# A loop over expert jobs: half of the next expert's first matrix is split a job ahead, its squares two jobs ahead, and its weights are asked for in two jobs

## The chip, the cores and the metric

The kernel runs on one core of one Trainium2 chip. The metric is the device time of one execution in microseconds (us), the median of several runs. The profile is one execution taken by the hardware profiler on that core. PE is TensorE (PEld its weight loads), DVE is VectorE, ACT is ScalarE, POOL is GpSimd, and SP is SyncE, which here only issues DMAs and reads registers.

## The reference, cut to what matters

```python
# attention: 4 x 8 heads, 768 tokens, head size 48
for t in range(S):
    cur = einsum('bhd,bhe->bhde', u * k_t, v_t)
    y_t = einsum('bhd,bhde->bhe', r_t, state + cur)
    state = w * state + einsum('bhd,bhe->bhde', k_t, v_t)
# mixture of experts on x = y as 3072 rows of 384; 8 experts, hidden size 1024
logits = x @ w_gate + modality_bias[modality_id]
e_idx = argmax(logits); gate_w = softmax(logits)[e_idx]
for e in range(E):
    h = maximum(x[mask] @ w1[e], 0.0)
    out[mask] = gate_w * (h @ w2[e])
```

The bias decides nearly all of the choices. With these inputs three experts have tokens: 1569, 1354 and 149.

## The kernel before, in words

**Attention and the first expert.** For about 200 us the attention runs in 24 units, and between them the kernel sends each token's row to a table in DRAM by expert and works off tiles of 128 rows of the first expert (`s_up`, `s_high`, `s_low`, `s_down`). What is left over is put into a table of jobs by `jobs()` (lines 837 to 947): a chain of small DVE instructions, drawn on piece by piece between other work, which ends in a product `jd`, a PE matmul `ptab` (line 939) and the copy to `tab`. A job is 128 rows of one expert. For each job the table holds the first row of its tokens (ROW), which expert to load (MORE) and a code: 4 says that the expert changes at this job, 8 that it changes at the next one, and 1 that the job is the one ahead of a change to the third or a later expert.

**The numbers.** Matrices are float32 in DRAM and are used as a pair of float16: `whi` (ACT, `broad`, line 1019) and the remainder `wlo` (DVE, `rest`, line 1023), both scaled by a power of two that comes from the sum of squares of the weights (`ws` for the first matrix, `wsb` for the second). `raw` holds the float32 weights of the next expert: columns 0 to 3071 are the first matrix, the rest the second. Activations are pairs too: `hh` (ACT, `relu_high`, line 1084) and `hl` (DVE, `relu_low`, line 1088). `F0 // 3` is 512 columns, `F0` 1536, `F2` 1920, `WC` 3072.

**The loop** (line 1660) goes over jobs 1 to 13 here, job 0 stands ahead of it (lines 1605 to 1622). Every engine runs its own program through the loop, in the written order; only SP, ACT and DVE take the branches. A job on PE is three groups of the first product (`raise_`, line 1074: features 0 to 3, 4 and 5, 6 and 7; for each, the `whi` terms come first and the `wlo` terms after them; 72 matmuls of 128 columns) with the small matmul `pw` (line 982, it sums the squares) behind the second group, then 16 matmuls of 384 columns of the second product (`high_terms`, line 1150; `wlo` of features 5 to 7 come last), and, at the top of the next round, 8 more with `hl` (`low_terms`, line 1158). In this order a round does:

- `finish_up()`: `relu_low` of features 4 to 7 of the job before (DVE).
- `take_in`: POOL copies the activations `xn` that a DMA has brought to `mxT` and the row numbers `mn` to `mt`. `turn` (line 1064): SP asks for `xn` of the job after this one.
- At a change, `go_on()`: the rest of the first matrix is split. In the job ahead of a change to the third expert, `by_both`: three of six squares on ACT, three on DVE.
- `low_terms` and `put` of the job before (ACT scales the result to `otb`, POOL scatters it to `out`).
- At a change, the first 1920 columns of the second matrix (`undo` writes `wf`, then blocks of 960). Then `due` (lines 1216 and 1217: `fac`, `ids`), `raise_` and `relu_high` of the first group, `raise_` of the second, `pw`.
- At a change, the last 1152 columns of the second matrix, and `relu_low` of features 0 to 3 behind them; in every other job `relu_low` and the five small instructions from the sums to `ws` and `wsb`.
- `next_load`: SP asks for both halves of the expert after this one, once the splits have read `raw`.
- `relu_high` of the second group, `raise_` and `relu_high` of the third, `begin()` if the next job is a change (the first 512 columns of `whi`), and `high_terms`.

```python
for g, span in enumerate(spans): ...         # job 0
with tc.For_i(1, nj, 1, ...) as i, ...:
    finish_up()
    take_in(nc.gpsimd)
    self.turn(0, self.at(ROW, i, E * CAP, SP, 1), mn, xn)
    with tc.If(code % 8 > 3) as begun:
        go_on()
    with begun.Else():
        with tc.If(code % 2 > 0):
            by_both(squares)
    self.low_terms(po)
```

Here job 0 and job 1 belong to the first expert, job 2 is the change to the second (11 jobs, 2 to 12), job 13 the change to the third, whose last 64 or fewer rows follow behind the loop as a half job (`h_up("z", ...)` and what follows, lines 1696 to 1712).

Of the kernel before, what the change touches and what calls it, by code (L numbers as in the profile page):

```python
# [18 lines left out]
P = 128  # L19
# [6 lines left out]
E = 8  # L26
# [43 lines left out]
class _Kernel:  # L70
# [766 lines left out]
    def jobs(self):  # L837
# [77 lines left out]
        v.reduce_sum(f, eq[:, :, 1:], axis=AX.X)  # L915
        v.reduce_sum(g, eq[:, :, 2:], axis=AX.X)
        yield
        v.scalar_tensor_tensor(field[:, SEEN : SEEN + 1], jr[:, 0:1], self.linep, field[:, ROW : ROW + 1], ALU.add, ALU.subtract)

# [4 lines left out]
        b = new("jbit", [P, 1])  # L924
        v.scalar_tensor_tensor(b, f[:, now], 4.0, g[:, soon], ALU.mult, ALU.add)
        mr = new("mr", [P, E - 1])
        v.tensor_mul(mr, eq[:, 1, 1:], nx[:, 1:])
# [291 lines left out]
    def run(self):  # L1219
# [386 lines left out]
        for g, span in enumerate(spans):  # L1606
            self.raise_(ph[g], *span)
            self.relu_high(ph[g], *span)
            if g == 0:
                self.relu_low(ph[g], *span)  # L1610
                self.scales("1")

        def finish_up():
            for g in (1, 2):
                self.relu_low(ph[g], *spans[g])

# [12 lines left out]
        def blocks(m, *at):  # L1629
            for lo, hi in zip(at, at[1:]):  # L1630
                self.broad(m, lo, hi)
                self.rest(m, lo, hi)

        def begin():
            self.broad(0, 0, F0 // 3)

        def go_on():
            self.rest(0, 0, F0 // 3)
            blocks(0, F0 // 3, F0, F0 + F0 // 2, WC)

# [7 lines left out]

        def next_load():
            more = self.at(MORE, i, 2 * E - 1, SP)  # L1650
            with tc.If(more > 0):
                self.load(more % E, 2, 0, 1)

# [6 lines left out]
        with tc.For_i(1, nj, 1, iteration_sync="reg_based") as i, tc.manual_schedule(engines={getattr(mybir.EngineType, e) for e in MS[:4]}):  # L1660
            finish_up()
            take_in(nc.gpsimd)
            self.turn(0, self.at(ROW, i, E * CAP, SP, 1), mn, xn)
            code = self.at(CODE, i, 15, AD)
            with tc.If(code % 8 > 3) as begun:
                go_on()
# [4 lines that stand above are left out]
            self.put(po, 0, "b")  # L1671
            with tc.If(code % 8 > 3):  # L1672
                self.undo()
                blocks(1, 0, F2 // 2, F2)
            self.due(m2, i)
            self.raise_(ph[0], *spans[0])
            self.relu_high(ph[0], *spans[0])
            self.raise_(ph[1], *spans[1])
            scaled = self.scales_("2")
            next(scaled)  # L1680
            with tc.If(code % 8 > 3) as first:
                blocks(1, F2, WC)
                self.relu_low(ph[0], *spans[0])
            with first.Else():
                self.relu_low(ph[0], *spans[0])
                for _ in scaled:
                    pass
                nc.vector.tensor_copy(self.wsb, self.ws[:, 1:])
            next_load()
            self.relu_high(ph[1], *spans[1])  # L1690
            self.raise_(ph[2], *spans[2])
            self.relu_high(ph[2], *spans[2])
            with tc.If(code > 7):
                begin()
            self.high_terms(po)
        take_in(nc.vector)
        finish_up()
        xhalf = self.xT[:, :, HP:P]
# [57 lines left out]
```

## Time and profile before

| | us |
|---|---|
| median of 3 runs | 330.07 (329.5, 331.53, 330.07) |
| the profiled execution: its own time | 330.74 |
| its span, first to last instruction | 329.0 |
| PE busy | 316.3 (96%) |
| DVE, POOL, ACT busy | 216.5, 186.8, 159.4 |
| the loop, from the first matmul of job 1 to the first behind the loop | 210.29 to 318.13 |

The granted TensorE clock was 0.99 on average and 1.00 in all of the loop. The span is what the rows below add up to; 1.74 us of the execution's own time lie outside it. Times within a row are from the start of the span.

### The profile page before, as it was taken

Reading aid. Unit: us, or ns where it says so; the run is one execution under the profiler, and the core shown is the slowest. Engines: PE = TensorE matmul, PEld = TensorE weight load, DVE = VectorE, ACT = ScalarE, POOL = GpSimd, SP = SyncE. Lnnn points to the kernel's source line nnn. Section 1 sums busy time; section 2 is a strip of 40 time slices with the busy share of each in tenths; the row PEclk is TensorE's granted clock in tenths of the full one; section 3 lists DMA queues with packets and bytes.
Section 4 is the critical chain, followed back from the end, with each engine's and each line's share of the span. In section 5 each row is a group of like instructions: output and inputs, shape, how many; then the busy total and the mean of one; then the engine's idle time right before and its main releaser. Section 6 shows DMA issues by size and latency. Waiting matters only on the chain. (4 is left out here: it accounts for less than half of the span.)

```text
span 329.0 us, 13842 instructions
## 1 busy us (share of the span) xinstructions
PE 316.3 (96%) x5056; PEld 259.2 (79%) x5056; DVE 216.5 (66%) x705; ACT 159.4 (48%) x380; POOL 186.8 (57%) x298
## 2 busy tenths in 40 slices
PE   7999999989999999999999999999999999999983
PEld 3888888889797988879789688876688888887652
DVE  6987789795999899978768841276222223336780
ACT  4667677662367546657834341283222222226731
POOL 8997698954999897656377723234323322222212
PEclk9999999998999999999999999999999999999998
DMA  7869688959949954899978332119822212221100
GB/s 214 251 174 303 188 248 269 185 109 243 339 121 221 283 178 90 180 272 258 202 155 260 114 87 57 35 44 339 122 60 48 48 48 48 60 57 26 48 16 28
DMA packets 50748, 49.59 MB, mean 151 GB/s; under 512 B 35573, under 2 KB 44315, under 8 KB 50448
## 3 DMA queue, kind: packets, MB, share of 16 engines
q1 hardware_dynamic: 46480, 37.93, 48.5%
q0 software_dynamic: 3168, 9.47, 8.3%
q10 hardware_dynamic: 1056, 1.58, 1.4%
q8 instruction: 30, 0.49, 0.7%
q14 instruction: 14, 0.11, 0.1%
HBM read 30.55 MB, written 11.44 MB: 128 GB/s over the span
## 5 line engine op out<-in xcount | busy, mean ns | idle before, releaser
L1082 PEld LDWEIGHTS <-whi 128*128 128x128 f16 x1248 | 71.0, 99 | 4.8 <-issue 2.0
L1156 PEld LDWEIGHTS <-hh 128*128 128x128 f16 x384 | 36.1, 98 | 24.1 <-issue 1.8
L1082 PE MATMUL phb<-mxT,whi 128*128 128x128 f16 x672 | 44.5, 219 | 1.0 <-POOL mxT L1620 0.8
L1091 DVE SCALAR_TENSOR_TENSOR hl<-phb,hh 128x256 f16<-128x256 f32 (+1 forms) x42 | 20.1, 509 | 34.7 <-PE pw L982 17.9
L1082 PEld LDWEIGHTS <-wlo 128*128 128x128 f16 x624 | 37.0, 99 | 0.3 <-DVE wlo L1025 0.3
L380 POOL TENSOR_TENSOR rc<-ud,powr 112x512 f32<-112x512 f32 x23 | 30.4, 1323 | 9.3 <-DMA ud<-in_pd 9.2
L1086 ACT ACTIVATE hh<-phb 128x256 f16<-128x256 f32 (+1 forms) x42 | 18.8, 453 | 30.8 <-PE L1082 12.5
L682 POOL DMA_INDIRECT rows<-row,posi x24 | 26.1, 1089 | 10.7 <-issue 9.1
L1082 PE MATMUL phs<-mxT,whi 128*128 128x128 f16 x480 | 31.1, 223 | 0.9 <-DMA mxT<-rows 0.9
L458 DVE TENSOR_TENSOR at<-psc,mask 128x512 f32<-128x512 f32 x48 | 31.6, 680 | 0.1
L452 PE MATMUL psc<-rc,kc 64*128 64x128 f32 (+1 forms) x384 | 28.6, 285 | 0.8 <-DVE rc L380 0.4
L1161 PEld LDWEIGHTS <-hl 128*128 128x128 f16 x192 | 18.4, 98 | 13.6 <-issue 1.7
L564 ACT ACTIVATE row<-py,sx 128x384 f16<-128x384 f32 x24 | 13.9, 581 | 30.4 <-DVE sx L338 22.5
L452 PEld LDWEIGHTS psc<-rc,kc 64*128 64x128 f32 (+1 forms) x384 | 23.7, 187 | 3.8 <-issue 1.7
L1050 POOL TENSOR_TENSOR seenb<-otb,putb 128x1 int32<-128x1 int32 x13 | 3.8, 295 | 39.7 <-ACTq L1672 31.0
L487 PE MATMUL py<-kv,at 128*64 128x48 f32 x768 | 26.4, 222 | 0.0
L1156 PE MATMUL po<-wlo,hh 128*128 128x384 f16 x112 | 25.2, 326 | 1.1 <-DVE wlo L1025 1.1
L1082 PE MATMUL phb<-mxT,wlo 128*128 128x128 f16 x336 | 25.8, 219 | 0.2 <-DVE wlo L1025 0.2
L487 PEld LDWEIGHTS py<-kv,at 128*64 128x64 f32 x768 | 25.0, 138 | 0.5
L1620 POOL COPY mxT<-xn 128x768 f16<-128x768 f16 x13 | 10.8, 828 | 25.5 <-PE L1156 17.9
L1156 PE MATMUL po<-whi,hh 128*128 128x384 f16 x112 | 25.1, 326 | 0.0
L1039 ACT ACTIVATE otb<-po,fac 128x384 f32<-128x384 f32 x13 | 7.5, 577 | 34.8 <-PE phb L1082 31.6
(317 smaller groups left out, 690.5 us busy)
## 6 DMA issues: line engine op xcount, KB each, us to landing
ud<-in_pd SPq DMA_DIRECT2D x24, 384.0 KB, 4.9
kv<-in_pt SPq DMA_DIRECT2D x24, 384.0 KB, 4.6
raw<-in_w SPq DMA_DIRECT2D x12, 512.0 KB, 4.9
raw<-in_w SPq DMA_DIRECT2D x2, 1536.0 KB, 7.6
r<-in_pt SPq DMA_DIRECT2D x10, 192.0 KB, 6.2
rows<-pad ACTq DMA_DIRECT2D x1, 1544.0 KB, 6.8
rows<-row,posi POOLq DMA_INDIRECT x24, 5.0
xn<-rows SPq DMA_TRANSPOSE x14, 3.0
```

The costliest lines, as they stand in the source:

```text
L380: return (engine or nc.gpsimd).tensor_mul(u["rc"][:R, s], u["rT"][:, s], self.powr[:R, s])
L452: nc.tensor.matmul(u["ps"][j][:, pr * P : (pr + 1) * P], u["kc"][r, pr, :], u["rc"][r, pr, :], start=True, stop=True)
L458: return nc.vector.tensor_mul(u["at"][:, j * NPR : (j + 1) * NPR, :], u["ps"][j].rearrange("p (q t) -> p q t", q=NPR), self.mask.unsqueeze ...
L487: nc.tensor.matmul(py[t, sl], u["at"][:, j * NPR + pr, t], u["v"][:, sl], start=c == h == 0, stop=h == H - 1 and i >= BARE, skip_group_che ...
L564: self.nc.scalar.activation(u["x16"][:, :DM], u["x"], AF.Copy, scale=u["g"]["sx"][:, b : b + 1])
L682: i = nc.gpsimd.indirect_dma_start(out=self.rows, out_offset=bass.IndirectOffsetOnAxis(ap=u["posi"][:, b : b + 1], axis=0), in_=u["row"][: ...
L1082: self.nc.tensor.matmul(ph[:, q * n : (q + 1) * n], w[:, c0 : c0 + P], x[:, xq, :], start=i == q == 0, stop=i == len(terms) - 1, skip_grou ...
L1086: self.nc.scalar.activation(self.hh[:, f0 : f0 + fb, t * P : (t + 1) * P], p3, AF.Relu)
L1091: self.nc.vector.scalar_tensor_tensor(self.hl[:, f0 : f0 + fb, r], p3, 0.0, self.hh[:, f0 : f0 + fb, r], ALU.max, ALU.subtract)
L1156: self.nc.tensor.matmul(po[:, :DM], self.hh[:, f, t * P : (t + 1) * P], w[:, c0 : c0 + DM], start=n == 0, stop=False)
L1161: self.nc.tensor.matmul(po[:, :DM], self.hl[:, f, t * P : (t + 1) * P], self.whi[:, c0 : c0 + DM], start=False, stop=f == FB - 1)
L1620: take_in = lambda e: (e.tensor_copy(self.xT[:, :, :P], xn), e.tensor_copy(m2[:, 0, :], mn[:, 0, :]))
```

## The change

The table's code says 1 two jobs ahead of a change if the expert in between has more than three jobs (`far`), else one job ahead as before. `relu_low` of features 4 to 7 stands in its own round. `begin()` splits 1536 columns, `whi` and `wlo`, in the job ahead of a change, and `go_on()` only the other 1536. `pw` stands behind the third group, and the scales are worked out only in the job with the squares. The first half of an expert's weights is asked for in the job of the change, the second half in the job after it, behind that job's `turn`.

```diff
         v.reduce_sum(g, eq[:, :, 2:], axis=AX.X)
-        yield
+        dq, far = new("dq", [P, E - 2]), new("far", [P, 1])
+        v.tensor_sub(dq, eq[:, 3, 2:], eq[:, 2, 2:])
+        yield
+        v.scalar_tensor_tensor(dq, jc[:, 1 : E - 1], 3.5, dq, ALU.is_gt, ALU.mult)
+        yield
+        v.reduce_sum(far, dq, axis=AX.X)
...
         v.scalar_tensor_tensor(b, f[:, now], 4.0, g[:, soon], ALU.mult, ALU.add)
+        yield
+        v.tensor_add(b, b, far)
...
             self.relu_high(ph[g], *span)
+            self.relu_low(ph[g], *span)
             if g == 0:
-                self.relu_low(ph[g], *span)
                 self.scales("1")
...
         def begin():
-            self.broad(0, 0, F0 // 3)
+            blocks(0, 0, F0 // 3, F0)
         def go_on():
-            self.rest(0, 0, F0 // 3)
-            blocks(0, F0 // 3, F0, F0 + F0 // 2, WC)
+            blocks(0, F0, F0 + F0 // 2, WC)
...
-        def next_load():
-            more = self.at(MORE, i, 2 * E - 1, SP)
+        def next_load(job, half):
+            more = self.at(MORE, job, 2 * E - 1, SP)
             with tc.If(more > 0):
-                self.load(more % E, 2, 0, 1)
+                self.load(more % E, 2, half)
...
-            finish_up()
             take_in(nc.gpsimd)
             self.turn(0, self.at(ROW, i, E * CAP, SP, 1), mn, xn)
+            next_load(i - 1, 1)
             code = self.at(CODE, i, 15, AD)
...
             self.raise_(ph[1], *spans[1])
+            with tc.If(code % 8 > 3):
+                blocks(1, F2, WC)
+            self.relu_low(ph[0], *spans[0])
+            next_load(i, 0)
+            self.relu_high(ph[1], *spans[1])
+            self.raise_(ph[2], *spans[2])
             scaled = self.scales_("2")
             next(scaled)
-            with tc.If(code % 8 > 3) as first:
-                blocks(1, F2, WC)
-                self.relu_low(ph[0], *spans[0])
-            with first.Else():
-                self.relu_low(ph[0], *spans[0])
+            self.relu_high(ph[2], *spans[2])
+            self.relu_low(ph[1], *spans[1])
+            self.relu_low(ph[2], *spans[2])
+            with tc.If(code % 2 > 0):
                 for _ in scaled:
                     pass
                 nc.vector.tensor_copy(self.wsb, self.ws[:, 1:])
-            next_load()
-            self.relu_high(ph[1], *spans[1])
-            self.raise_(ph[2], *spans[2])
-            self.relu_high(ph[2], *spans[2])
             with tc.If(code > 7):
                 begin()
             self.high_terms(po)
         take_in(nc.vector)
-        finish_up()
```

## Rows read from the trace of the kernel before

**Rows 1.** Busy time by stretch; one stretch per job, columns headed in the first line.

```profile
core 0: us, PE busy (x) PEld busy (x) DVE busy (x) ACT busy (x) POOL busy (x), PEclk, DMA share, GB/s
...
218.24:227.62 9.38, 8.66 (x99) 6.25 (x98) 8.60 (x12) 5.98 (x9) 4.98 (x4) 1.00 0.57 195
227.62:236.51 8.89, 8.11 (x98) 6.40 (x97) 2.33 (x10) 2.46 (x5) 2.24 (x5) 1.00 0.96 212
...
244.46:252.40 7.94, 7.94 (x98) 6.39 (x97) 2.33 (x10) 1.95 (x4) 2.28 (x5) 1.00 0.20 47
...
300.07:308.60 8.53, 8.16 (x99) 6.31 (x97) 5.98 (x16) 5.54 (x10) 2.61 (x5) 1.00 0.20 48
308.60:318.13 9.53, 7.65 (x92) 5.56 (x90) 8.35 (x11) 6.73 (x10) 1.83 (x2) 1.00 0.04 12
```

**Rows 2.** Timeline of PE: start, us, what, [idle time before it <- releaser].

```profile
225.63 0.65 PE L1156 MATMUL po<-wlo,hh 128*128 128x384 f16 x3 [0.64 <-DVE wlo L1025]
226.32 1.46 PE L1161 MATMUL po<-whi,hl 128*128 128x384 f16 x8
...
236.51 1.50 PE L1082 MATMUL phb<-mxT,whi 128*128 128x128 f16 x24 [0.79 <-POOL mxT L1620]
...
303.62 0.17 PE L982 MATMUL pw<-wssq,onesb 128*128 128x6 bf16 x1 [0.36 <-DVEq L1672]
...
318.13 0.81 PE L1161 MATMUL po<-whi,hl 128*128 128x384 f16 x4 [0.76 <-PEq L1752]
```

**Rows 3.** Timeline of SP, jobs 2 and 3: issue times of the DMAs.

```profile
221.44 4.59 SPq L965 DMA_DIRECT2D raw<-in_w  x2
227.46 2.23 SPq L1068 DMA_TRANSPOSE xn<-rows  x1
```

**Rows 4.** The tile xn from 220 to 240 us: from issue to landing.

```profile
DMA to landing us min/median/max: 3.0/5.5/8.0
```

**Rows 5.** Timeline of DVE in job 12, the last of its three squares.

```profile
302.24 1.23 DVE L1647 CUSTOM_DVE_ANT_0 squares<-raw 128x1024 f16<-128x1024 f32 x1
```

**Rows 6.** Timeline of ACT: the end of job 1, job 2, and job 12.

```profile
215.28 0.72 ACT L1021 ACTIVATE whi<-raw,ws 128x512 f16<-128x512 f32 x1
216.81 2.80 ACT L1021 ACTIVATE whi<-raw,ws 128x1024 f16<-128x1024 f32 x3 [0.81 <-PE po L1156]
...
222.44 1.25 ACT L1021 ACTIVATE whi<-raw,wsb 128x1152 f16<-128x1152 f32 x1
...
303.28 0.60 ACT L1086 ACTIVATE hh<-phb 128x512 f16<-128x512 f32 x1 [0.40 <-PE phb L1082]
```

**Rows 7.** Timeline of DVE in job 13 and behind the loop.

```profile
308.81 3.81 DVE L1025 SCALAR_TENSOR_TENSOR wlo<-raw,ws,whi 128x512 f16<-128x512 f32 x4 [0.60 <-SPq L1651]
...
315.00 0.14 DVE L1217 TENSOR_TENSOR ids<-mt,seenj 128x1 int32<-128x1 int32 x1
315.25 1.42 DVE L1025 SCALAR_TENSOR_TENSOR wlo<-raw,wsb,whi 128x1152 f16<-128x1152 f32 x1
316.58 0.68 DVE L1091 SCALAR_TENSOR_TENSOR hl<-phb,hh 128x512 f16<-128x512 f32 x1
...
318.58 0.74 DVE L1091 SCALAR_TENSOR_TENSOR hl<-phb,hh 128x256 f16<-128x256 f32 x2
```

**Rows 8.** DVE by line and shape, 210 to 318 us: xcount | busy, mean ns.

```profile
L1025 DVE SCALAR_TENSOR_TENSOR wlo<-raw,ws,whi 128x1024 f16<-128x1024 f32 x2 | 2.6, 1282 | 0.0
...
L1025 DVE SCALAR_TENSOR_TENSOR wlo<-raw,ws,whi 128x512 f16<-128x512 f32 x2 | 1.5, 753 | 1.2 <-DVE hl L1091 0.6 <-SPq L1651 0.6
```

**Rows 9.** Timeline of DVE in job 2.

```profile
223.59 0.65 DVE L1217 TENSOR_TENSOR ids<-mt,seenj 128x1 int32<-128x1 int32 x1
224.17 1.41 DVE L1025 SCALAR_TENSOR_TENSOR wlo<-raw,wsb,whi 128x1152 f16<-128x1152 f32 x1
```

**Rows 10.** Timeline of POOL in job 2.

```profile
223.30 0.93 POOL L1620 COPY mxT<-xn 128x768 f16<-128x768 f16 x1
```

**Rows 11.** Timeline of DVE, the last step of the job table.

```profile
195.50 0.32 DVE L936 TENSOR_TENSOR jd<-field,id 40x160 f32<-40x160 f32 x1
```

**Rows 12.** Timeline of PE, the matmul of the job table.

```profile
198.36 0.54 PE L939 MATMUL ptab<-jd,ones 40*128 40x160 f32 x2
```

More of the change, by code (lines that the diff above doesn't have):

```diff
@@ L1608, in run @@
             self.relu_high(ph[g], *span)
+            self.relu_low(ph[g], *span)
             if g == 0:
-                self.relu_low(ph[g], *span)
                 self.scales("1")
-        def finish_up():
-            for g in (1, 2):
-                self.relu_low(ph[g], *spans[g])
         xn = m.tile([P, 2 * DC, P], F16, name="xn", bufs=1)
```

## The prediction

> **What bounds the kernel now.** I read the busy times by stretch first, with one stretch per job of the loop [rows 1]. A plain job takes 7.94 us and PE is busy for all of it: nothing that only makes DVE, ACT or SP faster can shorten it. Four jobs are longer. Job 2 (change to the second expert) takes 9.38, job 3 8.89, job 12 8.53, and job 13, up to the first matmul behind the loop, 9.53. The first three are 1.44, 0.95 and 0.59 over a plain job. The first matmul behind the loop would come 6.64 us after the start of job 13 if nothing waited (from a plain job: its last 8 matmuls take 1.30 of the 7.94), so job 13 is 2.89 over. Together 5.9 us is all that this change can win in the loop.
>
> Then I looked at PE's timeline for what it waits for there [rows 2]. In job 2 it is `wlo` of the second matrix (0.64), and `low_terms` starts right behind `hl`. In front of job 4 it is `mxT` (0.79 idle). In job 12 it is the branch with the squares (0.36 in front of `pw`). At the end of job 13 it is the end of the loop (0.76). Below, R is the start of a job's first matmul: R2 = 218.24, R3 = 227.62, R12 = 300.07, R13 = 308.60 [rows 1].
>
> **Job 12: the squares.** The last square ends at 302.24 + 1.23 = 303.47, R12 + 3.40 [rows 5], and `pw`, which stands behind the second group, waits for it. In the changed kernel the squares stand in job 11 (the second expert has 11 jobs, more than 3.5, so `far` holds) and `pw` stands behind all 72 matmuls, near R + 4.0: 0.6 after the squares. So job 11 should not wait and job 12 becomes plain. Next late is the first `relu_high` of job 11: in job 12 it ended at 303.88, R12 + 3.81 [rows 6], just ahead of the second product at R + 4.04 (7.94 less three times the 1.30 of 8 matmuls), so the cover is 0.2 us. Gain 0.3 (if that slips) to 0.59; I take 0.58, since the row is on the good side.
>
> **Job 3: the loads.** SP issues both halves of the third expert from 221.44; the second issue ends at 226.03, since it waits for the last split, and `turn` for job 4 comes at 227.46 behind it [rows 3]. Its `xn` took 8.0 us to land, against 3.0 for another one [rows 4]: 235.46, and the copy to `mxT` and job 4 wait for it. In the changed kernel only the first half is in front of that `turn`, and the second half is issued behind it. With `turn` issued no later than before and 3.0 to land, `xn` is there at about 230.5 and the copy can't start before the third group of job 3 is done, R3 + 4.04 = 231.7; even 2 us more behind the rest of the first half cost nothing. The `turn` for job 5 now stands behind the second half; with the full 8.0 to land from about 234 it arrives at 242, just when job 5 needs it (R3 + 2 x 7.94 = 243.5 less 0.9 for the copy). What becomes late next is nothing. Gain 0.6 to 0.95; I take 0.9.
>
> **Job 13: the splits.** DVE is the chain there [rows 7]: four splits of the first matrix from R13 + 0.21 to R13 + 4.02; `wf`, two splits of 960 columns and `due` up to 315.25 (2.63); the split of 1152 (1.33 to the next start); `hl` of features 0 to 3 until 317.26; PE starts 0.87 later, behind the end of the loop. The change takes the splits of 512 and 1024 columns, 0.75 and 1.28 [rows 8], into the end of job 12, where DVE has nothing else. ACT must give `whi` first: 512 columns at about R13 - 2.9 as at the end of job 1 (215.28, 2.96 ahead of R2 [rows 6]), then 1024 in about 1.05, until R13 - 1.2. So DVE's split of 1024 runs from about R13 - 1.15 to R13 + 0.13. Then the engine has to go round the loop and read the job's code: ACT needed 1.53 from one start to the next there (215.28 to 216.81 [rows 6]), and by the same 1.53 DVE starts again at R13 + 0.4. From there by the durations above: the other two of the four splits 1.9 (R + 2.3), 2.63 (R + 4.95), 1.33 (R + 6.3), `hl` 0.68 (R + 7.0). Now `hl` of features 4 to 7 stands in front of the end of the loop: 0.74 more, which stood behind it, hidden beside PE [rows 7]. R + 7.7, and 0.87 to PE: R + 8.6 in place of 9.53. Without the gap at the top of the loop it is R + 8.3. ACT can hold it up: it gave the last 1152 columns at R2 + 5.45 in job 2 [rows 6], and gains between nothing and 0.8 by the same rearrangement; at nothing the last split starts 0.5 later, R + 9.1. Gain 0.4 to 1.25; I take 0.85. So sooner `hl` is no gain here but takes back part of one.
>
> **Job 2: the splits.** The same chain would put the end of the first `hl` at R2 + 7.0 and `low_terms` 0.13 later, where it was at 226.32, R2 + 8.08 [rows 2]: 0.9. But here POOL's copy of `xn` for job 3 falls between the splits: it ran from 223.30 to 224.23 [rows 10], the split of 1152 began at 224.17, and `ids`, 0.14 in job 13 [rows 7], took 0.65 [rows 9]. The copy can't run before the third group is done, R2 + 4.04 at best; then a split of 960 runs, and the chain puts the gap of `due` in front of the split of 1152 at R2 + 4.7 to 4.95, just where a waiting copy would slip in. If the copy goes first, the split starts at R2 + 5.9 as before and nothing is won; if not, 0.9. I take the middle, 0.45. The Trainium skill has a rule for this pair ("SBUF — State Buffer", section "Who interferes with whom"): a VectorE instruction with two inputs in SBUF and a GpSimd instruction that reads SBUF exclude each other, and whoever is second waits for the whole of the first. The rows of job 2 agree; by the rule alone the gain of job 2 would be at its lower end, and my sum 2.35 in place of 2.8.
>
> **What costs.** The table gets four DVE instructions, each below the 0.32 of its last product, some 0.7 together. That product ended at 195.82 [rows 11], `ptab` ran at 198.36 behind the second product of a tile [rows 12]: 2.5 us of cover. Without it 0.7; I take 0. Each round has one more branch on ACT and DVE and one more register read and branch on SP. In a plain job DVE is busy 2.33 and ACT 1.95 of 7.94 [rows 1], and a whole pass over the top of the loop fitted into 1.53; I take 0, and the upper end is the slower rival below. The scales that plain jobs no longer work out, and `hl` in its own round, win nothing: PE did not wait there.
>
> **Sum.** 0.58 + 0.9 + 0.85 + 0.45 = 2.8 us. The profiled execution, 330.74 of its own time with a span of 329.0, would take 327.9. It lies 0.67 above the median of the runs shown, 330.07, whose spread is 329.5 to 331.5; I set the sum against the median: 327.3. The low ends give 1.3 (328.8), the high ends 0.59 + 0.95 + 1.25 + 0.9 = 3.7 (326.4). About 1%, 3.3 us, is what a measurement of this kernel can tell from no change.
>
> **Rivals.**
> (a) More: DVE has no gap at the top of the loop and POOL's copy falls beside no split, in both changes. 3.7 us, 326.4. For it: the end of job 1 and of job 12 are empty on DVE, and ACT's work starts earlier too. Against it: the rows of job 2, and that ACT did show a gap of 0.81 at the same place [rows 6]. Chance 0.24.
> (b) The change doesn't do what it says: `far` isn't set, the squares stay in job 12, and the scales that they feed come late for the splits of job 13 again. Then 0.58 and half of 0.85 are gone: 1.8 us, 328.3. Against it: 11 jobs are far above 3.5. Chance 0.08.
> (c) Slower: `pw` now stands last in front of the second product, in all 13 jobs, and waits for DVE to have passed its branches, as it did in job 12 (0.36 there, 0.59 with what followed [rows 1, 2]). If DVE, with one branch more and two `relu_low` moved ahead of the end of the round, passes later than R + 4.0, every job pays: 13 x 0.36 to 13 x 0.59 is 4.7 to 7.7, less the 2.2 of the other jobs: 332.6 to 335.6, middle 334.0. Against it: the point lies far off, since the pass over the top took ACT 1.53 and DVE's last work before it ends ahead of R + 7.94, so that 4 us and more are left. Chance 0.06.
>
> **How the numbers follow.** The sum has 0.62. Faster by over 1% is (a) and the edge of the sum's own range, 0.28; slower by over 1% is (c), 0.06; the rest, 0.66, is within 1%. The range takes in the sum's ends 326.4 and 328.8 and half a microsecond to a full one of what medians of three runs scatter: 325.8 to 329.6.
>
> **What would show it.** Right: job 12 at 7.94 with the squares in job 11 and no idle time at `pw` in either; job 4 starting without a wait, `xn` of job 4 landed by 232; the first matmul of jobs 2 and 13 on time and splits of 512 and 1024 columns on DVE ahead of them; at the end of job 13 two short `hl` on DVE as the last thing in front of the loop's end, and PE idle for over 0.8 there. Wrong: a plain job over 7.95; a wait of job 5 or 6 for `xn`; job 11 over 7.95; POOL's copy in job 2 starting late and stretching into job 3. The largest unknown is the meeting of POOL's copy and DVE's last split.

## The result, and the profile after

The changed kernel took 334.55 us in the median of five executions, the kernel before 330.07 on the same chip: a ratio of 1.0118 [1.0081, 1.0156], with the 95% interval in brackets. It is 1.2% slower; 327.3 was predicted, with a range of 325.8 to 329.6. A second series on another chip gave 1.0101 [1.0066, 1.0136]. Executions at a lower granted clock stay out of the ratios (here one of 342.98; the others took 332.44 to 334.99), and as the profiles of the two runs that put the scales back (below) are of such, with a clock of 0.80 in the first 50 us, only their loops, at 1.00, and tails are used.

The profiled execution took 332.44, with a span of 330.7. Its attention part happened to be 1.8 us shorter than in the profile of before, so I compare jobs, from the start of one job's first matmul (R) to that of the next; for job 13 to the first matmul behind the loop, and "tail" is from there to PE's end. "Second" is the profile of the second series. Line numbers are those of each run's own kernel: L1032 of the changed kernel is L1025 of the rows of before, L1089 is L1082.

| | job 2 | job 3 | job 11 | job 12 | job 13 | the other 9 together | tail |
|---|---|---|---|---|---|---|---|
| before | 9.38 | 8.89 | 7.94 | 8.53 | 9.53 | 71.5 | 5.66 |
| predicted | 8.93 | 7.99 | 7.94 | 7.95 | 8.68 | 71.5 | 5.66 |
| changed, first | 10.91 | 7.95 | 9.63 | 7.95 | 11.05 | 71.8 | 5.66 |
| changed, second | 10.21 | 7.94 | 8.92 | 7.95 | 10.36 | 71.5 | 7.22 |

Jobs 3 and 12 came out as predicted. Jobs 2 and 13, which were to be shorter, got longer, and job 11 took more than job 12 gave. Added up, the first profile's row is 3.5 over the kernel before. The second's is 2.7 over it, and 1.56 of that is the tail. Changed kernel, busy time by stretch; jobs 2, 3, 7, 11, 12 and 13, to be laid beside [rows 1]:

```profile
216.46:227.37 10.91, 8.92 (x98) 6.34 (x97) 8.96 (x13) 6.65 (x10) 4.54 (x4) 1.00 0.57 179
227.37:235.32 7.95, 7.95 (x99) 6.31 (x97) 1.83 (x5) 1.95 (x4) 2.50 (x6) 1.00 0.74 245
259.24:267.22 7.98, 7.98 (x99) 6.30 (x98) 1.84 (x5) 1.94 (x4) 2.28 (x5) 1.00 0.21 52
291.21:300.84 9.63, 8.46 (x98) 6.39 (x97) 5.95 (x16) 5.24 (x10) 3.39 (x5) 1.00 0.24 56
300.84:308.79 7.95, 7.95 (x100) 6.32 (x98) 2.56 (x6) 3.42 (x6) 2.28 (x5) 1.00 0.12 33
308.79:319.84 11.05, 7.69 (x90) 5.56 (x89) 8.37 (x13) 6.59 (x10) 2.44 (x2) 1.00 0.12 25
```

DVE's busy time in jobs 2 and 13 hardly changed (8.60 to 8.96, 8.35 to 8.37), and ACT's rose by 0.67 in job 2 and fell by 0.14 in job 13: the new time, about 1.5 in each, is mostly waiting and not work. Where PE waits, its timeline says (job 2, job 11, behind the loop; answers to [rows 2]):

```profile
220.04 0.51 PE L1089 MATMUL phb<-mxT,wlo 128*128 128x128 f16 x6 [0.41 <-DVE wlo L1032]
...
223.86 0.48 PE L1163 MATMUL po<-wlo,hh 128*128 128x384 f16 x2 [1.21 <-DVE wlo L1032]
...
295.19 0.51 PE L1089 MATMUL phb<-mxT,wlo 128*128 128x128 f16 x6 [0.79 <-DVE wssq L1649]
...
319.84 0.81 PE L1168 MATMUL po<-whi,hl 128*128 128x384 f16 x4 [2.19 <-PEq L1754]
```

ACT at the end of job 1 (answers to [rows 6]) and DVE there, in job 11 and at the loop's end (answers to [rows 9, 5, 7]):

```profile
213.89 0.38 ACT L1093 ACTIVATE hh<-phb 128x256 f16<-128x256 f32 x1 [0.70 <-PE po L1163]
215.01 3.50 ACT L1028 ACTIVATE whi<-raw,ws 128x512 f16<-128x512 f32 x4 [0.73 <-DVEq L1692]
```

```profile
214.31 0.42 DVE L1098 SCALAR_TENSOR_TENSOR hl<-phb,hh 128x256 f16<-128x256 f32 x1 [0.66 <-ACT hh L1093]
215.76 0.75 DVE L1032 SCALAR_TENSOR_TENSOR wlo<-raw,ws,whi 128x512 f16<-128x512 f32 x1 [1.03 <-ACT whi L1028]
216.88 1.28 DVE L1032 SCALAR_TENSOR_TENSOR wlo<-raw,ws,whi 128x1024 f16<-128x1024 f32 x1 [0.37 <-ACT whi L1028]
218.97 1.95 DVE L1032 SCALAR_TENSOR_TENSOR wlo<-raw,ws,whi 128x768 f16<-128x768 f32 x2 [0.80 <-ACT otb L1046]
...
220.90 2.91 DVE L1032 SCALAR_TENSOR_TENSOR wlo<-raw,wsb,whi 128x960 f16<-128x960 f32 x2
...
223.92 1.41 DVE L1032 SCALAR_TENSOR_TENSOR wlo<-raw,wsb,whi 128x1152 f16<-128x1152 f32 x1
...
289.06 0.42 DVE L1098 SCALAR_TENSOR_TENSOR hl<-phb,hh 128x256 f16<-128x256 f32 x1 [0.66 <-ACT hh L1093]
292.52 1.23 DVE L1649 CUSTOM_DVE_ANT_0 squares<-raw 128x1024 f16<-128x1024 f32 x1 [3.03 <-PE phb L1089]
...
316.87 1.35 DVE L1098 SCALAR_TENSOR_TENSOR hl<-phb,hh 128x512 f16<-128x512 f32 x3
```

L1692 is the condition around the scales, and "DVEq" is DVE's sequencer: ACT's first `whi` of job 1 waits 0.73 for an instruction of DVE that is not work but a condition. It starts at R2 - 1.45, against R2 - 2.96 before. Job 2's chain of splits starts from there. The line's own view (whole run) shows what waited for it:

```profile
L1692 DVEq COMPARE_BRANCH  x14: 75/119/128, 214.4 to 316.1; - x14
...
L1692 DVEq EVENT_SEMAPHORE  x12: 21/21/21, 214.9 to 318.3; - x12
...
  ACT whi L1028: 1.4, 2
```

The 12 are the jobs in which the block is skipped: 13 rounds less job 11. Where the block is skipped, DVE's queue has a semaphore instruction in place of the work left out. In job 1 DVE passed the branch itself at 214.4, while the last `hl` was still running; that `hl` ended at 214.31 + 0.42 = 214.73, the semaphore instruction came at 214.9, and ACT's `whi` started at 215.01. I read this as a wait for the engine's own unfinished work, behind which the semaphore is stepped that others count.

### The profile page after: what moved, and what is told of

The parts are those of the page before. It is cut to its first block, busy times and chain, and to the rows that moved or that the text cites. A ratio compares the mean times of both kernels' runs of the same rounds, so it can differ in the third digit from the quotient of the medians.

```text
span 330.7 us, 13969 instructions
## 1 busy us (share of the span) xinstructions
PE 316.6 (96%) x5056; PEld 257.6 (78%) x5056; DVE 208.2 (63%) x659; ACT 159.5 (48%) x380; POOL 190.2 (58%) x298
## 3 DMA queue, kind: packets, MB, share of 16 engines
q0 software_dynamic: 3168, 9.47, 8.1%
## 5 line engine op out<-in xcount | busy, mean ns | idle before, releaser
L1089 PEld LDWEIGHTS <-whi 128*128 128x128 f16 x1248 | 70.3, 98 | 3.3 <-ACT whi L1028 0.5
L1163 PEld LDWEIGHTS <-hh 128*128 128x128 f16 x384 | 35.0, 97 | 26.3 <-issue 3.2
L1089 PE MATMUL phb<-mxT,whi 128*128 128x128 f16 x672 | 44.7, 219 | 0.3 <-ACT junk L975 0.2
L1098 DVE SCALAR_TENSOR_TENSOR hl<-phb,hh 128x256 f16<-128x256 f32 (+1 forms) x42 | 21.0, 511 | 28.1 <-ACT hh L1093 19.6
L1089 PEld LDWEIGHTS <-wlo 128*128 128x128 f16 x624 | 36.3, 98 | 2.5 <-DVE wlo L1032 1.1
L380 POOL TENSOR_TENSOR rc<-ud,powr 112x512 f32<-112x512 f32 x23 | 31.3, 1361 | 5.7 <-DMA ud<-in_pd 5.6
L1089 PE MATMUL phs<-mxT,whi 128*128 128x128 f16 x480 | 30.1, 219 | 0.0
L1089 PE MATMUL phb<-mxT,wlo 128*128 128x128 f16 x336 | 25.8, 219 | 1.7 <-DVE wssq L1649 0.8
L1223 DVE TENSOR_SCALAR fac<-mt,wf 128x1 f32<-128x1 f32 x14 | 3.0, 213 | 38.3 <-DVEq L1674 30.7
L1057 POOL TENSOR_TENSOR seenb<-otb,putb 128x1 int32<-128x1 int32 x13 | 4.9, 376 | 37.1 <-ACTq L1674 29.0
```

What stands on the lines that cost most here:

```text
L380: return (engine or nc.gpsimd).tensor_mul(u["rc"][:R, s], u["rT"][:, s], self.powr[:R, s])
L1089: self.nc.tensor.matmul(ph[:, q * n : (q + 1) * n], w[:, c0 : c0 + P], x[:, xq, :], start=i == q == 0, stop=i == len(terms) - 1, skip_grou ...
L1098: self.nc.vector.scalar_tensor_tensor(self.hl[:, f0 : f0 + fb, r], p3, 0.0, self.hh[:, f0 : f0 + fb, r], ALU.max, ALU.subtract)
L1163: self.nc.tensor.matmul(po[:, :DM], self.hh[:, f, t * P : (t + 1) * P], w[:, c0 : c0 + DM], start=n == 0, stop=False)
```

## The experiments

All jobs that moved, by the same measure as above. Jobs 1 and 4 to 10 took 7.94 or 7.95 in these runs, but for job 1 of after_lows_as_before (11.89) and of candidate_five (8.61):

| run | job 2 | job 3 | job 11 | job 12 | job 13 | tail | ratio to before |
|---|---|---|---|---|---|---|---|
| before_split_loads | 9.58 | 7.95 | 7.94 | 9.85 | 9.52 | 5.66 | 1.0014 [0.9964, 1.0063] |
| before_squares_sooner | 9.38 | 9.35 | 8.48 | 7.94 | 9.64 | 5.66 | 1.0012 [0.9978, 1.0046] |
| before_lows_sooner | 9.48 | 7.94 | 7.94 | 8.73 | 9.96 | 7.24 | 0.9992 [0.9953, 1.0031] |
| before_lows_and_big_begin | 9.34 | 7.94 | 7.94 | 8.85 | 9.65 | 5.66 | 0.9998 [0.9952, 1.0044] |
| after_lows_as_before | 12.25 | 9.57 | 11.24 | 11.16 | 8.73 | 5.66 | 1.0402 [1.0341, 1.0462] |
| after_scales_behind_begin | 10.45 | 7.95 | 8.92 | 7.94 | 11.11 | 5.66 | 1.0116 [1.0048, 1.0185] |
| after_small_begin | 10.22 | 8.59 | 8.92 | 8.17 | 10.71 | 6.93 | 1.0071 [1.0051, 1.0091] |
| after_load_later_in_round | 10.14 | 7.94 | 8.69 | 7.94 | 10.22 | 5.66 | 1.0047 [1.0014, 1.0079] |
| changed_scales_as_before | 9.41 | 7.94 | 9.74 | 7.94 | 9.09 | 7.23 | 1.0008 [0.9972, 1.0043] |
| changed_scales_and_load_branch | 9.33 | 7.94 | 8.85 | 7.94 | 8.98 | 7.24 | 0.9978 [0.9942, 1.0014] |
| candidate_one | 9.40 | 7.94 | 7.94 | 8.54 | 9.52 | 5.66 | 0.9958 [0.9926, 0.9990] |
| candidate_two | 10.59 | 7.94 | 8.81 | 7.94 | 9.93 | 5.66 | 1.0037 [1.0008, 1.0065] |
| candidate_five | 10.44 | 7.95 | 7.94 | 8.55 | 9.52 | 5.66 | 1.0049 [1.0010, 1.0089] |
| candidate_six | 9.47 | 7.94 | 8.38 | 7.94 | 9.59 | 5.66 | 1.0007 [0.9976, 1.0038] |

**The loads alone** (before_split_loads).

```
+        def next_load(job, half): ...
             self.turn(0, self.at(ROW, i, E * CAP, SP, 1), mn, xn)
+            next_load(i - 1, 1)
...
-            next_load()
+            next_load(i, 0)
```

> The kernel before with one part of the change: the two halves of the next expert are asked for in two jobs, each behind its own read and branch on SP. Theory A (the loss of the change comes from what DVE must finish in front of the branches, the loop's back-edge and the loop's end): only job 3 changes, 8.89 to about 7.95; all other jobs as before, relu_high of features 4 and 5 at R + 3.5; 0.94 less, about 329.1 us. Theory B (the second read and branch on SP holds up the loop's engines in every round): relu_high of features 4 and 5 slips to R + 4.3 in plain jobs too, plain jobs take 7.97 to 8.01, jobs 2 and 13 some 0.4 longer; about 330.3 us.

Job 3 went to 7.95 and `relu_high` stayed at R + 3.5 (theory A's marks, not B's), but the total did not move: job 12 grew by 1.32, which neither theory had. DVE's timeline there, its first square:

```profile
297.44 1.22 DVE L1647 CUSTOM_DVE_ANT_0 squares<-raw 128x1024 f16<-128x1024 f32 x1 [2.13 <-SPq L1651]
```

It waits for SP's sequencer (SPq) at the condition around the load (L1651), R12 + 0.64 instead of R12 - 0.59. No load takes place there: the reader of `raw` waits until SP has passed a block that might write it. In the program the new block stands ahead of the squares and on SP behind `turn`. [Rows 7 and 8] had the same releaser, "0.60 <-SPq L1651", already; I read it as a detail.

**The squares alone** (before_squares_sooner: the seven lines of the table that set `far`, nothing in the loop).

```
+            dq, far = new("dq", [P, E - 2]), new("far", [P, 1])
...
+            v.tensor_add(b, b, far)
```

> The kernel before with one part of the change: the flag that puts the squares of the third expert into job 11 instead of job 12; pw stays behind the second group. Theory A: in the order of before DVE passes the back-edge before its hl of features 4 to 7, so the squares start at R - 0.6 also in job 11 and end at R + 3.4: job 12 is plain (7.95) and job 11 takes what job 12 took (8.5), not 9.63; total 330.1, no change. Theory C (squares in job 11 are dear whatever stands in front of them, since they meet another load or another wait there): job 11 takes over 9 us, total over 330.9.

Theory A's numbers: 8.48 and 7.94. Job 3's 9.35 is `xn` again, which landed later than in the profile of before. What I had not foreseen: DVE was 0.90 ahead in job 13 (last split until R + 7.17 instead of R + 8.06), and the job still took 9.64. The view of the loop's end (L1759 there, 306 to 318 us) shows the last engine:

```profile
L1759 POOLq DRAIN  x2: 111/3244/6376, 309.8 to 316.3; - x2
...
L1759 DVEq DRAIN  x1: 953/953/953, 314.0 to 314.0; - x1
```

DVE is through at 314.0 + 0.95 = 315.0, POOL at 309.8 + 6.38 = 316.2. In the kernel before POOL came to 317.5 and DVE to 317.4 (L1752, 306 to 319 us):

```profile
L1752 POOLq DRAIN  x2: 111/2799/5487, 312.0 to 317.7; - x2
...
L1752 DVEq DRAIN  x1: 957/957/957, 316.4 to 316.4; - x1
```

So two waits ended nearly together there, and PE's line in [rows 2], which names PEq L1752, tells of neither.

**`hl` put back** (after_lows_as_before).

```
             with tc.If(code % 8 > 3) as begun:
                 go_on()
             with begun.Else():
+                finish_up()
...
-            self.relu_low(ph[1], *spans[1])
-            self.relu_low(ph[2], *spans[2])
...
             with tc.If(code > 7):
+                finish_up()
                 begin()
```

> The changed kernel, with hl of features 4 to 7 put back to the top of the next round (in front of the squares there), except where a split of the first matrix is begun: there it stays ahead of the splits. Theory A: in job 11 the squares start near R - 0.6 again and the job falls from 9.63 to 8.0 - 8.5 (1.1 to 1.7 less); the loop's end costs 0.7 to 1.5 less (job 13 from 11.05 to 9.6 - 10.3); jobs 2 and 12 hardly change; together 2 to 3 less than the changed kernel, 331.5 to 332.5. Theory B: jobs 11 and 13 stay within 0.3 of the changed kernel's, 334.5.

A miss for both: 343.63. With `hl` inside conditional blocks, jobs 0 to 3, 11 and 12 are 0.9 to 3.9 us longer than in the changed kernel's first profile. PE in front of job 2:

```profile
221.23 1.44 PE L1168 MATMUL po<-whi,hl 128*128 128x384 f16 x4 [3.09 <-DVE wlo L1032]
```

These matmuls of `low_terms` need `hl` of features 4 to 7, which had ended at 216.24. They start 5.0 later, released by a split: I read it as a wait for the condition whose one branch holds `hl` and whose other branch holds the splits. Only job 13 got shorter, to 8.73, by more than theory A had.

**The branches exchanged** (after_scales_behind_begin).

```
+            with tc.If(code > 7):
+                begin()
             with tc.If(code % 2 > 0):
                 ... (the scales)
-            with tc.If(code > 7):
-                begin()
```

> The changed kernel with the conditional scales moved behind the beginning of the split (the two branches change places). Theory A: ACT's first broad of jobs 1 and 12 no longer waits for DVE to pass the scales' branch (0.73 of its delay), so the chain of splits starts 0.7 sooner: jobs 2 and 13 each 0.4 to 0.7 shorter, job 11 and the loop's end as in the changed kernel; 1.0 less, 333.4. Rival D (the chain of splits in jobs 2 and 13 is set by POOL's copy and by ACT, not by the start of broad): jobs 2 and 13 within 0.2 of the changed kernel's.

Theory A's cause was there, its gain was not. The first split started 0.8 sooner than in the second profile (R - 2.22 for R - 1.40), but now the skipped block stands behind the split of 1024: the 768 start at R + 2.04, later than R + 1.80, and job 13 took 11.11. Moved, the block was paid at the next place.

**The changed kernel again** (changed_again, no edit).

> The changed kernel itself, on another chip and in other executions. Theory E (the late relu_high in the plain jobs of its first profile, R + 4.3 instead of R + 3.5, belongs to that execution, since the kernel before with the loads split and the changed kernel with two branches exchanged have as many branches and show R + 3.5): plain jobs 7.95 and relu_high at R + 3.5 to 3.6 in this profile, while job 2 stays over 10.4, job 11 over 8.8, job 13 near 11.1. Theory B (it belongs to the program): plain jobs 7.97 to 8.01 and R + 4.3 again.

Theory E: plain jobs 7.95, `relu_high` at R + 3.6. The late `relu_high` of the first profile (R + 4.3 in every job, some 0.7 of jobs 2, 11 and 13 each) belongs to that execution; what makes it is open. Without it jobs 2 and 13 are 0.83 longer than before, job 11 0.98. And here the tail took 7.22. Its stretches, 318.97 being the first matmul behind the loop:

```profile
308.61:318.97 10.36, 7.37 (x91) 5.56 (x89) 8.05 (x12) 5.91 (x9) 2.43 (x2) 1.00 0.04 12
318.97:320.50 1.53, 1.53 (x19) 1.19 (x20) 1.08 (x6) 0.00 (x0) 0.33 (x2) 0.68 0.04 11
320.50:322.50 2.00, 2.00 (x42) 2.00 (x40) 0.23 (x1) 0.38 (x1) 0.04 (x1) 0.50 0.00 0
```

Behind 2.19 of idle PE the granted clock was 0.50, the 1.2 GHz level, for about 3 us, and the tail lost 1.56. The first profile had the same idle time and a clock of 1.00. The mean granted clock of the nine executions here was 0.987, of the kernel before in the same series 0.994, so a part of the second series' 1.0% may be such stretches; only the one profile shows where they lie.

**The small beginning** (after_small_begin).

```
         def begin():
-            blocks(0, 0, F0 // 3, F0)
+            self.broad(0, 0, F0 // 3)
         def go_on():
-            blocks(0, F0, F0 + F0 // 2, WC)
+            self.rest(0, 0, F0 // 3)
+            blocks(0, F0 // 3, F0, F0 + F0 // 2, WC)
```

> The changed kernel, with only the broad of 512 columns in the job ahead, as before; DVE has no split there. Theory F (a split of DVE inside the last conditional block holds DVE's way round the loop: block end, back-edge, code load and branch begin only when the split has ended and take 1.4 to 1.9): DVE's first split of job 2 starts at R + 0.2 to 0.4 and all four follow one another, done by R + 4.1, as in the kernel before; job 2 falls from 10.4 - 10.9 to 9.3 - 9.9. Job 13 falls less than job 2's amount is over 9.38, to 10.7 - 11.0, since the loop's end still stands behind three hl and two branch ends. Job 11 unchanged (8.9 - 9.6). Rival G (the two splits ahead are worth what the prediction gave them, and the loss of job 2 comes from the load of half a matrix and POOL's copy): job 2 gets longer, over 10.9.

Neither: job 2 took 10.22, as with the large one (10.21). The 0.73 of ACT behind the scales (L1693 there) stayed, so the four splits ran from R - 0.05 to R + 3.83. The splits ahead are neither the loss nor, in this kernel, a gain. Job 3's 8.59 has a wait of PE of 0.47 for DVE at the condition around the squares (L1671 there), a skipped block again.

**The load's branch moved** (after_load_later_in_round).

```
             self.turn(0, self.at(ROW, i, E * CAP, SP, 1), mn, xn)
-            next_load(i - 1, 1)
...
+            next_load(i - 1, 1)
             next_load(i, 0)
```

> The changed kernel, with the read and branch for the second half moved from the top of the round to right in front of the one for the first half. On SP the order stays the same (behind turn); what changes is that the squares stand ahead of it in the program, so they no longer wait until SP has passed that branch in their own round. Theory H (two things hold DVE's squares of job 11 at R + 1.2: SP's branch behind turn, and DVE's own way round the loop behind its hl): freeing one of them wins little, job 11 shortens by 0 to 0.4 and its squares start no sooner than R + 0.6. Rival I (SP's branch alone): squares at R - 0.6, job 11 at 8.0 to 8.5. Jobs 2, 3 and 13 as in the changed kernel.

Theory H in the job, 8.69 (8.92 in the second profile), though the squares started a little sooner than it allowed, at R + 0.37. What still held them there, `hl` and the skipped blocks by theory H, was not taken out one by one.

**First candidate** (candidate_two: candidate_one's loads, and of the changed kernel the squares, pw's place and the scales' condition).

> Of the change, what should be free of its losses: loads in two jobs with both branches in the middle of the round, squares two jobs ahead, pw behind the third group, scales under a condition; hl of features 4 to 7 and the beginning of the split as before. It presumes that an expert in the middle has at least three jobs, as here. Theory A with H: job 3 at 7.95, squares of job 11 from R - 0.6 to R + 3.4 and job 11 at 8.0 to 8.4, job 12 at 7.95, jobs 2 and 13 at 9.4 and 9.5; 1.2 less than the kernel before. Rival (pw, or the conditional scales, cost something by themselves): job 11 over 8.5 or plain jobs over 7.97.

A miss. pw did not stall, but the scales' block stands behind `hl` of features 0 to 3, and `hl` of 4 to 7, at the top of the next round, came late in job 11 and job 2:

```profile
229.11 0.83 PE L1168 MATMUL po<-whi,hl 128*128 128x384 f16 x4 [0.74 <-DVE hl L1098]
```

**`hl` sooner alone, and with the splits ahead** (before_lows_sooner; before_lows_and_big_begin).

```
-            finish_up()
...
             self.relu_high(ph[2], *spans[2])
+            self.relu_low(ph[1], *spans[1])
+            self.relu_low(ph[2], *spans[2])
             with tc.If(code > 7):
```

and for the second run `begin()` and `go_on()` of the change.

> The kernel before with one part of the change: hl of features 4 to 7 in its own round, ahead of the back-edge and of the loop's end. Theory A: plain jobs stay 7.95; at the loop's end DVE has two hl more to do (0.74), so job 13 goes from 9.52 to 10.2 - 10.3; in job 12 the squares wait until DVE has been round the loop behind its hl, start at R + 0.0 to + 0.4 instead of R - 0.59, and the job grows from 8.53 to 9.1 - 9.5; job 2 within 0.1 of 9.38. Together 1.3 to 1.8 more than the kernel before. Rival J (the engine passes its branches beside its work, so hl in its own round is free but for the loop's end): job 12 at 8.5, 0.7 more in all.

> The same and the second part: the splits of 512 and 1024 columns in the job ahead. Here no conditional scales stand between hl and the beginning, so ACT's broad need not wait for DVE. Theory K (DVE's way from the end of the block round the loop to the next split takes 2.0 on its sequencer; beside the split of 1024 only 1.3 of it is hidden; and at the loop's end POOL's drain, 4.0 behind its scatter, ends as late as DVE in the kernel before, so that DVE alone can win nothing there): job 2 has its four splits done by R + 2.8 to 3.2, where they were done by R + 2.98 before, and stays 9.3 to 9.6; job 13 has them done by R + 3.0 instead of R + 4.0, its first hl ends about 1.0 sooner, and yet the job takes 9.5 to 10.2. Rival L (the prediction's term): jobs 2 and 13 some 0.45 and 0.85 shorter than in the run with hl alone, 8.9 and 9.4.

`hl` alone: job 12 + 0.20, job 13 + 0.43, less than theory A had, and nothing that the totals show. With the splits ahead: four splits done by R + 2.94 in job 2, whose length is unchanged; in job 13 by R + 3.53, first `hl` 0.69 sooner, the job 9.65. Theory K's picture with smaller amounts. These two parts together do not make a loss, so it had to lie in what they meet in the changed kernel.

**Two more candidates** (candidate_one: the loads in two jobs, both branches behind the squares; candidate_five).

```
             (candidate_one, in the middle of the round)
-            next_load()
+            next_load(i - 1, 1)
+            next_load(i, 0)
```

> The kernel before with the loads split over two jobs, both reads and branches in the middle of the round, behind the squares in the program. It presumes that an expert in the middle has at least three jobs, as here. Theory H: job 3 at 7.95 (0.95 less), and job 12 at 8.53 as in the kernel before, not 9.85 as with the branch at the top of the round, since the squares now wait for the branch of the round before; all else as before; 0.95 less in all. Rival M (job 12's 9.85 came from the split loads themselves): job 12 over 9.5 and no gain in all.

As theory H had it, job by job: 7.94 and 8.54. 327.98 against 329.22 in its series, the only run whose interval lies below 1. It is one of fourteen variants, measured in one series, so 0.4% is to be taken with care; what job 3 is worth varies too (see below).

> Candidate one, and the squares in job 11 with pw behind the third group; the scales stand in the other branch of the split's condition and are worked out only in the job ahead of a change, so that no skipped block stands behind DVE's last work. Theory H with A: job 3 at 7.95, job 11 at 7.95 to 8.1, job 12 at 7.95, job 2 at 9.4, job 13 at 9.5 to 9.7 (POOL's drain); 1.4 to 1.5 less than the kernel before. Rival (pw behind the third group stalls PE): job 11 over 8.3.

A miss in the total. Job 11 is plain at last with the squares in it, but scales that start behind a late pw hold up `hl` of features 4 to 7 in jobs 1 and 12 (8.61 and 8.55), and job 2 starts 1.1 later on DVE.

**The scales put back** (changed_scales_as_before; changed_scales_and_load_branch adds the moved load branch).

```
+            scaled = self.scales_("2")
+            next(scaled)
+            with tc.If(code % 8 > 3) as first:
                 blocks(1, F2, WC)
+                self.relu_low(ph[0], *spans[0])
+            with first.Else():
+                self.relu_low(ph[0], *spans[0])
+                for _ in scaled: ...
...
-            with tc.If(code % 2 > 0):
-                for _ in scaled: ...
```

> The changed kernel with one thing put back: pw stands behind the second group again and the scales are worked out in the other branch of the split's condition, in every job that is no change, so that no skipped block of scales stands on DVE behind hl. Loads, squares, hl of features 4 to 7 and the splits ahead as changed. Theory N (the largest loss is that skipped block: ACT's broad waits until DVE has passed it, and the loop's end too): ACT's first broad starts 2.9 ahead of R2 again, job 2 falls from 10.2 - 10.9 to 9.3 - 9.5 and job 13 from 10.4 - 11.1 to 9.6 - 9.8; job 11 stays long, 9.2 to 9.9, since SP's branch still holds the squares and pw waits for them. Rival A (the splits ahead and hl themselves): job 2 and job 13 stay over 10.0.

Theory N in jobs 2 and 11 and in ACT's start; job 13, 9.09, is 0.5 below what it had. Jobs 2, 11 and 13, and ACT at the end of job 1 (R2 = 226.55):

```profile
226.55:235.97 9.42, 8.58 (x100) 6.33 (x98) 7.82 (x12) 5.33 (x8) 4.88 (x4) 1.00 0.57 183
299.52:309.27 9.75, 8.29 (x100) 6.42 (x98) 6.51 (x16) 4.27 (x10) 3.06 (x5) 1.00 0.16 41
...
317.21:326.30 9.09, 7.17 (x91) 5.54 (x89) 7.31 (x12) 5.30 (x8) 2.44 (x2) 1.00 0.05 14
```

```profile
223.65 3.51 ACT L1028 ACTIVATE whi<-raw,ws 128x512 f16<-128x512 f32 x4
```

No wait in front of `whi`, 2.9 ahead of R2. The loads, the squares, `hl` and the splits ahead are still as changed, and the kernel is level with the one before. The run moves `pw` together with the scales, and no run parts the two; that it was the skipped block is read from L1692 in front of `whi`, and from the loop's end (below).

> The same, and the branch of the second half put behind the squares in the program. All parts of the change are in, with two places altered. Theory N with H: jobs 2 and 13 as in the run beside it, job 11 at 8.5 to 8.9, job 12 at 7.95: 0.4 to 0.9 less than the kernel before. Rival A: over the kernel before.

Job 11 falls by 0.89 to 8.85 and stays 0.91 over a plain job, so SP's branch and what is left, DVE's order and `pw` in front of the third group, cost about the same there. 0.22% less than before is inside the interval; the five jobs add up to 1.2 less in the profile, and the tail, 1.6 longer there, took more than that back.

**Last candidate** (candidate_six: candidate_one, the squares two jobs ahead, and pw at the top of the round).

> Candidate one (loads in two jobs, the branch behind the squares) with the squares two jobs ahead and pw at the top of the round, ahead of the squares in the program, so that it takes the sums of the job before and waits for nothing. It presumes that an expert in the middle has at least four jobs, as here. Theory: job 3 at 7.95, job 11 at 7.95 to 8.1, job 12 at 7.95, jobs 2 and 13 at 9.4 and 9.5; 1.4 to 1.5 less than the kernel before, 0.5 less than candidate one. Rival (the squares stall PE in job 11 also without pw, by the weights' second halves, which wait for DVE's branch): job 11 at 8.3 or more and no gain over candidate one.

The rival: job 11 at 8.38 and no gain in the total, though jobs 11 and 12 together are 0.16 less than in candidate_one. Candidate_one stays the only version clear of the kernel before, by 0.4%.

## Why the prediction was wrong, point by point

**Job 3, 0.9: right, in part by luck.** 0.94, with the order on SP as the prediction had it. SP's issues and `xn` from 220 to 240 us, beside [rows 3 and 4]:

```profile
221.15 0.34 SPq L972 DMA_DIRECT2D raw<-in_w  x1
222.89 1.45 SPq L1075 DMA_TRANSPOSE xn<-rows  x1
...
226.85 0.34 SPq L972 DMA_DIRECT2D raw<-in_w  x1
```

```profile
DMA to landing us min/median/max: 3.1/4.6/6.2
```

`turn` came 4.5 ahead of R3 instead of 0.2, so that even 6.2 to landing cost nothing. But the term is not a constant of the kernel: with both loads asked for at once, job 3 took 7.94 in before_lows_sooner and 9.35 in before_squares_sooner. What it is worth lies between 0 and 1.4, by execution, and the profile of before happened to show 0.95.

**Job 12, 0.58: right; job 11, 0: wrong.** The step that failed is "job 11 should not wait". I took the squares' times over from job 12, R - 0.59 to R + 3.40. In the changed kernel DVE comes to them at R + 1.31 in the first profile, R + 0.61 in the second: `hl` of features 4 to 7, the skipped blocks, the way back to the top of the loop and the read of the code lie ahead, and SP's new branch as well, which was worth 0.23 of job 11 when it was moved in the changed kernel and 0.89 when it was moved with the scales put back. PE pays 0.79, released by DVE's squares, and smaller waits. 1.0 to 1.7 in place of 0, and more than the 0.58 of job 12.

**Jobs 13 and 2, 0.85 and 0.45: wrong in sign.** Two steps failed. First, "512 columns at about R13 - 2.9" and "DVE starts again at R13 + 0.4": measured R - 1.5 and R + 2.4 in the first profile, R - 2.2 and R + 1.7 in the second. The skipped scales took 0.73 of it, the first execution's late `relu_high` 0.7, and from the start of DVE's split of 1024 to its next split, on the way round the loop, it was 2.0 to 2.1, not ACT's 1.53. With the scales put back `whi` does start at R - 2.9, and job 13 takes 9.09: about half of the 0.85, since the next split still starts only at R + 1.0 (2.0 after the one of 1024) and `hl` and the loop's end stand behind. Second, "0.87 to PE" at the loop's end. From the end of the last `hl` to PE it is 319.84 - 318.22 = 1.62. The runs part this: 0.80 with no skipped block behind `hl` (before_lows_sooner), 1.08 with that of `begin()` alone (scales put back), 1.45 with that of the scales alone (after_small_begin). The sum also took DVE for the only one that the loop's end waits for: POOL's drain came as late in the kernel before, and DVE's 0.90 in before_squares_sooner bought nothing.

For job 2 I also laid job 13's chain over it, though its four splits had been done by R + 2.98 before, 1.0 sooner than in job 13; so there was nothing to win by starting two of them ahead, 9.33 to 9.41 at best: the low end of my bounds. What its length does follow is the end of the fourth split. The job ends 6.39 to 6.45 behind it in the kernel before (R + 2.98, length 9.38), in both profiles of the changed one (4.46 and 10.91, 3.76 and 10.21), with the small beginning (3.83, 10.22) and with the scales put back (3.02, 9.41).

The meeting with POOL's copy, the largest unknown by the prediction, came at another place: the copy (221.90 to 222.79) fell beside the two splits of 960 columns in job 2, which took 2.91 there against 2.35 in job 13. The trace agrees there with the rule of the Trainium skill ("SBUF — State Buffer", section "Who interferes with whom"). It cost 0.56, in place of the 0.51 that `ids` lost to the copy before (0.65 for 0.14, [rows 9 and 7]), so it is not the loss of job 2.

**The branches, 0: the term that decided.** "A whole pass over the top of the loop fitted into 1.53; I take 0" looked at how much time DVE has in a plain job. Plain jobs did cost nothing (7.94 or 7.95 in the second profile). The cost is where someone waits for an engine to have passed a block: ACT for DVE at the scales, DVE for SP at the load, PE for DVE at the loop's end. Rival (c) had this mechanism, a DVE that passes its branches late, but put it at pw in every job, where 4 us of room were left, and gave it 0.06. It should have been asked at each place that reads what the moved or new block may write: `ws` (ACT's broad), `raw` (the squares), the loop's end.

**Rivals (a) and (b)** fell: `far` was set, and job 2 had no gain to give.

## What to carry to other kernels

In this kernel a conditional block cost time where it was skipped behind work, and not in the plain jobs. Before adding one, list what it may write, and for each reader what the engine has still to finish when it reaches the block. Put such a block where the engine's queue is empty, or, as with the scales put back, into the other branch of a condition that is passed anyway; exchanging two blocks here only moved the wait. And where a loop's end or another meeting of all engines sets the time, work out the arrival of every engine: the trace's line names one releaser, and a second engine may come as late.

## What the runs showed of the hardware that was not expected

- POOL's drain (its wait at the loop's end) ended 4.0 behind its last scatter, in the kernel before (scatter 312.07 + 1.43, drain until 317.5) as in before_squares_sooner (310.33 + 1.87, until 316.2) and in the changed kernel (312.37 + 1.60, until 318.0).
- A load that is not executed can still hold the reader of its buffer: the squares of before_split_loads waited 2.13 us for SP to pass the condition of a load that did not take place.
- The clock behind the loop's end: 0.50 (1.2 GHz) for some 3 us in the second profile of the changed kernel and 1.00 in the first, with the same 2.19 of idle PE ahead. In before_lows_sooner it fell to 0.50 behind only 1.36 of idle PE. Three other runs have tails of 6.93 to 7.24 too, against 5.66 in the rest. What decides it in an execution is open.
